# Transposing q and k by the DMA crossbar instead of TensorE, from the ninth unit on

## The chip, the core and the metric

The kernel runs on one core of one Trainium2 chip. A core has five engines with queues of their own, which meet at semaphores: TensorE (PE; its weight loads are PEld), VectorE (DVE), ScalarE (ACT), GpSimd (POOL) and SyncE (SP). Here SP issues all loads, ACT issues the stores of the results, and 16 DMA engines carry them out. An engine takes its instructions in the order of the program: one that waits holds up all behind it. The metric is the device time of one execution in microseconds (us), as the median of several runs.

## What is computed

Eight heads of retention (attention with a decay in place of the softmax), then a feed-forward block with a squared ReLU.

```python
scores = scale * np.matmul(q, k.transpose(0, 1, 3, 2))      # q, k, v: (8, 8, 576, 64) float32
gamma = 1.0 - 2.0 ** (-5.0 - np.arange(H))
Dmat = np.where(rel >= 0, gamma[:, None, None] ** rel, 0.0)  # rel = pos_i - pos_j
attn = np.matmul(scores * Dmat, v)
x = attn.transpose(0, 2, 1, 3).reshape(B * S, H * D)         # (4608, 512)
h = x @ w_in                                                 # (512, 2048)
r = np.maximum(h, 0.0)
out = (r * r) @ w_out                                        # (4608, 512) float32
```

## The kernel before

**Units.** A unit is 128 rows of the sequence with all 8 heads. A batch of 576 rows gives four full units, and the last 64 rows of two batches make one "tail" unit together: 36 units, nine for each pair of batches; unit 8 is the first tail. Heads go in pairs (NP = 4), so that a pair of 64 columns fills 128 partitions.

**What one unit does.** SP loads k, q and v as fp32 (L289, tails in two halves L292; five buffers). POOL casts k and q to fp16 (k16, q16; L338, L342) and multiplies v by its decay into vp (L347, four buffers, freed by the output matmuls four units back). For units 0 to 3 ACT casts q. PE transposes k and q, 128x128 at a time, four blocks each, into one PSUM tile psT (L374). ACT copies the k part to kT in two halves with zeros between, one for each head of a pair (L380, L383), and DVE copies the q part to qT (L387). From these PE makes the scores psc (L447, eight matmuls); DVE masks them into rT (L455). PE multiplies rT by vp and q by the running state R into psO (L479, L483). The state comes from k16 and vp (psS, L408) and two DVE steps (L422, L427). DVE scales psO into xT (L498).

**Feed-forward.** Units form groups of 1, 1, 2, 2, 2 and then 4. For each group PE makes ph (L526, 64 matmuls), ACT applies ReLU into rl (L534), DVE squares it into gT (L539), PE makes po (L556, 16 matmuls of 512 columns per unit), ACT copies po to o (L564) and issues the store (L570).

**What sets the order.** The class Schedule holds each step as a task with an engine, a key, an assumed duration, what it depends on, and the buffers that it takes and frees. `emit` plays these tasks through once while the program is built: at each moment a free engine takes the ready task with the lowest key. The order found is what each engine's queue then holds. The keys are due times in units of one feed-forward matmul; `base` is a unit's own, and L = 32 keys are one unit. A step of the retention part runs beside the feed-forward matmuls of the group before. SP's tasks all have key 0, in one chain. WARM matmuls (L235) keep PE running while the first loads come.

Each DMA raises one of eight completion counters, taken in turn by loads and stores alike in the order of the program, and it waits until the DMA that had its counter before has landed.

The names that the change touches: `kTs`, `kqs`, `fk`, `fq`, `fx2`, `ck` and `cq` (the casts), `tk` and `tq` (the transposes), `e0`, `e1`, `eq` (the copies out of PSUM), `transposed`, and the counts in `Schedule(dict(...))`.

Of the kernel before, what the change touches and what calls it, by code (L numbers as in the profile page):

```python
# [15 lines left out]
class Schedule:  # L16
# [85 lines left out]
def kernel(  # L102
# [9 lines left out]
    nc = tc.nc  # L112
# [33 lines left out]
    st_pool = ctx.enter_context(tc.tile_pool(name="st", bufs=6))  # L146
# [101 lines left out]
    zeroed = [[]]  # L248
    for i in range(1, NB):
        zeroed.append([add_gated("POOL", i - 1, "k", 1.5,  # L250
                                 lambda i=i: (zero_kT(nc.gpsimd, i), zero_vp(nc.gpsimd, i)))])

    def make_bdec():

# [74 lines left out]
    def add_ret(u):  # L329
# [2 lines left out]
        base = (u - len(us)) * L  # L332
        early = u < ahead
        tail = [tail_pool, tail_dec] if kind == "tail" else []

        def fk():
            t = tile_of["k16", u] = cast.tile([P, H * D], FP16, name="k16", tag="k16")
            nc.gpsimd.tensor_copy(out=t, in_=tile_of["k32", u].rearrange("p h d -> p (h d)"))  # L338

        def fq():  # L340
            t = tile_of["q16", u] = cast.tile([P, H * D], FP16, name="q16", tag="q16")
            (nc.scalar.copy if early else nc.gpsimd.tensor_copy)(  # L342
                out=t, in_=tile_of["q32", u].rearrange("p h d -> p (h d)"))

        def fv():
# [3 lines left out]
                in0=tile_of["v32", u].rearrange("p (n a) d -> p n a d", a=2),  # L349
                in1=vdec[kind].rearrange("p (n a o) -> p n a o", a=2, o=1).to_broadcast([P, NP, 2, D]),  # L350
                op=ALU.mult)
        ck = add("POOL", base - L, 0.73, fk, deps=[loaded["k", u]], acq=("k16",))
        if early:
            cq = add("ACT", base - L, 0.6, fq, deps=[loaded["q", u]], acq=("q16",))
        else:
            cq = add("POOL", base - L + 1, 0.62, fq, deps=[loaded["q", u]], acq=("q16",))
# [8 lines left out]
        def ft(i, src):  # L365
# [8 lines left out]
                    nc.tensor.transpose(tile_of["ps" + src[0], u][:, i, hp, :],  # L374
                                        tile_of[src, u][:, hp * P:(hp + 1) * P], ident)
            return f
        kT = kTs[u % NB]

        def fe0():
            nc.scalar.copy(out=kT[0:64, :, 0, :], in_=tile_of["psk", u][0:64, 0])  # L380
# [4 lines left out]
        def feq():  # L385
            t = tile_of["qT", u] = work.tile([P, NP, P], FP16, name="qT", tag="qT")
            nc.vector.tensor_copy(out=t, in_=tile_of["psq", u][:, 1])  # L387
        prev = [T["score", u - NB]] if u >= NB else zeroed[u]
        tk = add("PE", base - 17.6, 0.22, ft(0, "k16"), deps=[ck] if early else [ck, cq], acq=("psT",))
        tq = add("PE", base - 17.5, 0.22, ft(1, "q16"), deps=[cq, tk], acq=("psc",) if early else ())  # L390
        sched.free("q16", [tq])
        e0 = add("ACT", base - 15.5, 0.58, fe0, deps=[tk if early else tq] + prev)
        e1 = add("ACT", base - 15.4, 0.58, fe1, deps=[e0])

        eq = add("DVE", base - 15.3, 0.42, feq, deps=[tq] if early else [tq, e1], acq=("qT",))
        if early:
            sched.free("psT", [e0, e1])
            sched.free("psc", [eq])
        else:
            sched.free("psT", [e0, e1, eq])  # L400


        if kind == "full":
            def fs():
                ps = tile_of["psS", u] = ps_one.tile([P, NP, 2, D], FP32, name="psS", tag="psS")
                for hp in range(NP):
                    vo = vps[u % NB].rearrange("p n (a d) -> p n a d", d=64)[:, hp, 0:3:2, :]
                    nc.tensor.matmul(ps[:, hp], lhsT=tile_of["k16", u][:, hp * P:(hp + 1) * P], rhs=vo,  # L408
                                     start=True, stop=True)
            s = add("PE", base + 0.5, 0.22, fs, deps=[ck, cv], acq=("psS",))  # L410
            sched.free("k16", [s, tk])
            if c == 0:
                def fr():
                    Rn = tile_of["R", u] = st_pool.tile([P, NP, P], FP16, name="R", tag="R")
                    nc.vector.tensor_tensor(out=Rn, in0=tile_of["psS", u].rearrange("p n a d -> p n (a d)"),
                                            in1=bdec, op=ALU.mult)
                r = add("DVE", base + 1.5, 0.7, fr, deps=[s, made_bdec], acq=("R",))
                sched.free("psS", [r])
            else:
                def fr0():  # L420
                    tmp = tile_of["tmp", u] = work.tile([P, NP, P], FP32, name="stmp", tag="stmp", bufs=2)
                    nc.vector.tensor_tensor(out=tmp, in0=tile_of["psS", u].rearrange("p n a d -> p n (a d)"),  # L422
                                            in1=tile_of["R", u - 1], op=ALU.add)

                def fr():
                    Rn = tile_of["R", u] = st_pool.tile([P, NP, P], FP16, name="R", tag="R")
                    nc.vector.tensor_tensor(out=Rn, in0=tile_of["tmp", u], in1=bdec, op=ALU.mult)  # L427
                r0 = add("DVE", base + 1.5, 0.7, fr0, deps=[s, T["R", u - 1]])
                sched.free("psS", [r0])
                r = add("DVE", base + 1.6, 0.7, fr, deps=[r0], acq=("R",))  # L430
                T["Rread", u - 1].append(r0)
            T["R", u] = r
            T["Rread", u] = []
        else:
            sched.free("k16", [tk])


        sc = []
# [1 line left out]
        for half in range(2):  # L440
            for j in range(2):
                def f(half=half, j=j):
                    hp = 2 * half + j
                    if j == 0:
                        tile_of["psc", u, half] = ps_sc.tile([P, 2, 2, P], FP32, name="psc", tag="psc")
                    for a in range(2):
                        nc.tensor.matmul(tile_of["psc", u, half][:, j, a, :], lhsT=kT[:, hp, a, :],  # L447
                                         rhs=tile_of["qT", u][:, hp, :], start=True, stop=True)
                sc.append(add("PE", base + 5 + 2 * half + j + 0.6, 0.11, f, deps=[e0, e1, eq] + sc[-1:],
                              acq=("psc",) if j == 0 else ()))  # L450

            def fm(half=half):
                if half == 0:
                    tile_of["rT", u] = work.tile([P, NP, 2, P], FP16, name="rT", tag="rT")
                nc.vector.tensor_tensor(  # L455
                    out=tile_of["rT", u][:, 2 * half:2 * half + 2].rearrange("p n a i -> p (n a) i"),
                    in0=tile_of["psc", u, half].rearrange("p n a i -> p (n a) i"),
                    in1=mask[kind].rearrange("p (o i) -> p o i", o=1).to_broadcast([P, 4, P]),
                    op=ALU.mult)
# [13 lines left out]
        for hp in range(NP):  # L473
            def f(hp=hp):
# [6 lines left out]
                                     stop=(a == 1 and not inter))  # L481
                for n, (lo, hi, ru) in enumerate(inter):
                    nc.tensor.matmul(ps[:, hp, lo:hi], lhsT=tile_of["R", ru][:, hp, :],  # L483
                                     rhs=tile_of["qT", u][:, hp, lo:hi], start=False, stop=(n == len(inter) - 1))
# [134 lines left out]
```

## Time and profile before

| what | value |
|---|---|
| median of 3 runs (lowest to highest) | 336.01 us (335.69 to 336.94) |
| the profiled execution, its own time | 335.73 us |
| its span in the profile | 334.0 us |
| TensorE's granted clock | 1.00 in every stretch |
| transposes, L374 | 288 matmuls, 128x128 |
| scores, L447 | 288 matmuls, 128x128 |
| copies of kT, L380 and L383 | 36 and 36, 575 and 581 ns |
| copies of qT, L387 | 32 (and 4 more from another PSUM tile), 423 ns |
| casts of k and v's decay on POOL, L338 and L347 | 36 at 643 ns, 32 (full units) at 1049 ns |
| read from HBM, written | 36.70 MB, 9.44 MB |

The span is the time from the first to the last recorded event of the one profiled execution; the run's time is a little longer. A row of the timeline gives start, length, engine, line, operation, out<-in, size and count; a PE row's length has the last matmul's way through the array in it, so the start of the next row tells better when PE was free. In square brackets stands idle time of the engine ahead of the row, and what ended it. "SPq" is SP's queue: the time for which an issue held it.

### The profile page before, as it was taken

The numbers are of one execution on the slowest core, as the hardware profiler recorded it, in microseconds if no ns is written. First come the engines' busy times: TensorE is split into PE (matmuls) and PEld (weight loads), VectorE is DVE, ScalarE is ACT, GpSimd is POOL, SyncE is SP. The second block draws the span as 40 slices with busy tenths as digits, with TensorE's granted clock in tenths as the row PEclk, the third lists the DMA queues.
The fourth block names the chain that finished last, engine by engine and source line by source line (L and its number), as shares of the span: only waits on it lengthen the run. The fifth ranks groups of instructions, "written<-read, shape, count | busy, mean of one in ns | idle before, by whom it ended". The sixth has DMA issues, their size and how long they took to land.

```text
span 334.0 us, 6482 instructions
## 1 busy us (share of the span) xinstructions
PE 324.4 (97%) x2528; PEld 194.4 (58%) x2528; DVE 192.5 (58%) x367; ACT 159.9 (48%) x273; POOL 98.7 (30%) x141
## 2 busy tenths in 40 slices
PE   5999999899999999999999999999999999999996
PEld 2679655777755555555555555555555555554444
DVE  2596436887848843774388447843686357623500
ACT  4458843643446523662366226632663256414611
POOL 6834475657322222322222222312222110000000
PEclk9999999999999999999999999999999999999999
DMA  9999999999959958435544565453000120011013
GB/s 176 222 386 386 305 252 224 225 205 252 222 132 232 208 125 208 105 73 148 149 104 90 131 154 124 97 127 95 32 2 0 65 63 0 3 65 63 0 42 86
DMA packets 122158, 46.56 MB, mean 139 GB/s; under 512 B 113296, under 2 KB 113552, under 8 KB 122128
## 3 DMA queue, kind: packets, MB, share of 16 engines
q1 hardware_dynamic: 116736, 36.71, 50.1%
q10 hardware_dynamic: 5392, 9.44, 8.4%
q8 instruction: 20, 0.33, 0.4%
q14 instruction: 10, 0.08, 0.1%
HBM read 36.70 MB, written 9.44 MB: 138 GB/s over the span
## 4 chain that ended last, share of the span: by engine, by line
PE 86%; SPq 7%; DVE 3%; DMA 1%; issue 1%; POOL 0%; ACT 0%; POOLq 0%
PE ph L526 34%; PE po L556 33%; SPq L289 6%; PE psO L479 4%; PE psc L447 4%; PE psT L374 4%; PE warm L235 3%; PE psS L408 2%; PE psO L483 2%; DMA q<-in_q_dram 1%; SPq L292 1%; DVE rT L455 1%; DVE R L427 1%; DVE stmp L422 1%; POOL q L342 0%
## 5 line engine op out<-in xcount | busy, mean ns | idle before, releaser
L556 PE MATMUL po<-w_out,gT 128*128 128x512 f16 (+1 forms) x592 | 146.8, 373 | 0.8 <-POOL w_out L314 0.8
L526 PE MATMUL ph<-xT,w_in 128*128 128x512 f16 (+2 forms) x768 | 140.6, 326 | 0.0
L534 ACT ACTIVATE rl<-ph 128x512 f16<-128x512 f32 x144 | 85.6, 597 | 47.3 <-PE ph L526 42.8
L526 PEld LDWEIGHTS <-w_in 128*128 128x128 f16 x768 | 66.1, 98 | 39.0
L539 DVE TENSOR_TENSOR gT<-rl 128x512 f16<-128x512 f16 x144 | 71.1, 500 | 27.1 <-ACT rl L534 25.4
L556 PEld LDWEIGHTS <-gT 128*128 128x128 f16 x592 | 55.2, 98 | 42.2 <-issue 1.0
L380 ACT COPY kTb<-psT 64x512 f16<-64x512 f16 x36 | 20.7, 575 | 63.6 <-PE psT L374 59.8
L564 ACT COPY o<-po 128x512 f32<-128x512 f32 (+1 forms) x37 | 21.3, 575 | 56.1 <-PE po L556 55.7
L455 DVE TENSOR_TENSOR rT<-psc,mask_full 128x512 f16<-128x512 f32 x64 | 41.8, 684 | 6.7 <-PE psc L447 6.3
L347 POOL TENSOR_TENSOR vp<-v,vdec_full 128x512 f16<-128x512 f32 x32 | 33.6, 1049 | 34.4 <-PE psO L483 24.9
L342 POOL CAST q<-q 128x512 f16<-128x512 f32 x32 | 21.3, 666 | 68.4 <-PE psT L374 24.7
L338 POOL CAST k<-k 128x512 f16<-128x512 f32 x36 | 23.2, 643 | 42.5 <-issue 20.0
L479 PEld LDWEIGHTS <-vp 128*128 128x128 f16 x288 | 25.4, 98 | 16.3 <-issue 1.2
L479 PE MATMUL psO<-rT,vp 128*128 128x128 f16 x288 | 33.9, 219 | 0.4 <-DVE rT L455 0.2
L387 DVE COPY qT<-psT 128x512 f16<-128x512 f16 x32 | 13.5, 423 | 35.0 <-ACT kTb L383 34.9
L447 PEld LDWEIGHTS <-kTb 128*128 128x128 f16 x288 | 23.7, 98 | 15.3 <-issue 0.3
L447 PE MATMUL psc<-qT,kTb 128*128 128x128 f16 x288 | 31.5, 219 | 0.0
L422 DVE TENSOR_TENSOR stmp<-psS,R 128x512 f32<-128x512 f32 x24 | 16.5, 689 | 25.2 <-PE psS L408 25.0
L498 DVE TENSOR_TENSOR xT<-psO,gam_full 128x512 f16<-128x512 f32 x32 | 22.1, 690 | 9.5 <-PE psO L483 5.3
L483 PE MATMUL psO<-qT,R 128*128 128x128 f16 (+1 forms) x128 | 22.6, 212 | 0.0
L383 ACT COPY kTb<-psT 64x512 f16<-64x512 f16 x36 | 20.9, 581 | 0.6
L235 PE MATMUL warm<-junk,ident 128*128 128x512 f16 x48 | 15.0, 425 | 3.7 <-DVE junk L230 3.7
(57 smaller groups left out, 159.5 us busy)
## 6 DMA issues: line engine op xcount, KB each, us to landing
k<-in_k_dram SPq DMA_DIRECT2D x32, 256.0 KB, 4.7
q<-in_q_dram SPq DMA_DIRECT2D x32, 256.0 KB, 4.7
v<-in_v_dram SPq DMA_DIRECT2D x32, 256.0 KB, 4.8
out_dram<-o ACTq DMA_DIRECT2D x31, 256.0 KB, 2.1
wi<-in_moe_w_in_dram SPq DMA_DIRECT2D x4, 1024.0 KB, 10.7
wo<-in_moe_w_out_dram SPq DMA_DIRECT2D x4, 1024.0 KB, 9.3
out_dram<-o ACTq DMA_DIRECT2D x10, 128.0 KB, 2.4
k<-in_k_dram SPq DMA_DIRECT2D x8, 128.0 KB, 3.9
```

The source lines that it names most:

```text
L235: nc.tensor.matmul(warm_ps[0], lhsT=ident, rhs=junk, start=True, stop=True)
L338: nc.gpsimd.tensor_copy(out=t, in_=tile_of["k32", u].rearrange("p h d -> p (h d)"))
L347: nc.gpsimd.tensor_tensor(out=vo, in0=tile_of["v32", u].rearrange("p (n a) d -> p n a d", a=2), in1=vdec[kind].rearrange("p (n a o) -> p n ...
L447: nc.tensor.matmul(tile_of["psc", u, half][:, j, a, :], lhsT=kT[:, hp, a, :], rhs=tile_of["qT", u][:, hp, :], start=True, stop=True)
L455: nc.vector.tensor_tensor(out=tile_of["rT", u][:, 2 * half:2 * half + 2].rearrange("p n a i -> p (n a) i"), in0=tile_of["psc", u, half].re ...
L479: nc.tensor.matmul(ps[:, hp, :], lhsT=vps[u % NB][:, hp, a * 64:a * 64 + P], rhs=tile_of["rT", u][:, hp, a, :], start=(a == 0), stop=(a == ...
L483: nc.tensor.matmul(ps[:, hp, lo:hi], lhsT=tile_of["R", ru][:, hp, :], rhs=tile_of["qT", u][:, hp, lo:hi], start=False, stop=(n == len(inte ...
L498: nc.vector.tensor_tensor(out=tile_of["x", us[0]][:, :, s * P:(s + 1) * P], in0=tile_of["psO", u], in1=gam[kind], op=ALU.mult)
L526: nc.tensor.matmul(tile_of["ph", g, fb][:, j, :], lhsT=w_in16[:, m, fi * P:(fi + 1) * P], rhs=tile_of["x", us[0]][:, m, :], start=(m == 0) ...
L534: nc.scalar.activation(out=t, in_=tile_of["ph", g, fb], func=ACTF.Relu)
L539: nc.vector.tensor_tensor(out=t, in0=rl, in1=rl, op=ALU.mult)
L556: nc.tensor.matmul(tile_of["po", u, lo], lhsT=tile_of["g", g, fi // nf][:, fi % nf, s * P:(s + 1) * P], rhs=w_out16[:, fi, lo:hi], start=( ...
```

## The change

The program of units 0 to 7 stays, but for some buffer counts. From unit 8 on (XBAR = 8):

- POOL writes k twice: into a tile kq of 12 blocks of 128 columns, where blocks 0 to 7 hold the four pairs of k, each pair twice, once with the second and once with the first head's 64 columns left at zero; and as before into k16, for the state. It writes q into blocks 8 to 11. There are three kq tiles; DVE zeroes their k parts once at the start.
- SP issues one DMA that transposes all 12 blocks into a tile kqT (three buffers). It depends on both casts. Its key is -1, ahead of the loads, its assumed duration 2.0.
- psT and the copies kT and qT are gone; the scores and the state's part of the output read kqT.
- The casts of unit u wait for the transpose of unit u-3, which reads the same kq.
- Buffers: kT 4 to 3, R 6 to 5, rT 3 to 2, q16 4 to 2. The warm-up matmuls read the first kq instead of a tile of their own.

```diff
-    kTs = [const.tile([P, NP, 2, P], FP16, name=f"kTb{i}") for i in range(NB)]
+    NT = 3
+    kTs = [const.tile([P, NP, 2, P], FP16, name=f"kTb{i}") for i in range(NT)]
...
+    NK = 3
+    kqs = [const.tile([P, 3 * NP, P], FP16, name=f"kq{i}") for i in range(NK)]
+    nc.vector.memset(kqs[0][:, 0:2 * NP], 0.0)
     zero_kT(nc.vector, 0)
     zero_vp(nc.vector, 0)
+    for t in kqs[1:]:
+        nc.vector.memset(t[:, 0:2 * NP], 0.0)
...
+    XBAR = 8
-    sched = Schedule(dict(ff=3, psc=2, psT=1, psS=1, psO=1, ld=5, wst=4, k16=4, q16=4,
-                          qT=3, rT=3, x=3, rl=3, o=3, R=6))
+    sched = Schedule(dict(ff=3, psc=2, psT=1, psS=1, psO=1, ld=5, wst=4, k16=4, q16=2,
+                          qT=3, rT=2, x=3, rl=3, o=3, R=5, kqT=3))
...
-    junk = const.tile([P, 512], FP16, name="junk")
-    nc.vector.memset(junk, 0.0)
+    junk = kqs[0][:, 0:NP].rearrange("p n c -> p (n c)")
...
+        xbar = u >= XBAR
+        kq = kqs[u % NK]
         def fk():
+            if xbar:
+                nc.gpsimd.tensor_copy(
+                    out=kq[:, 0:2 * NP].rearrange("p (n a) (b d) -> p n (a b) d", a=2, d=64)[:, :, 0:4:3, :],
+                    in_=tile_of["k32", u].rearrange("p (n a) d -> p n a d", a=2))
             t = tile_of["k16", u] = cast.tile([P, H * D], FP16, name="k16", tag="k16")
...
         def fq():
+            if xbar:
+                nc.gpsimd.tensor_copy(out=kq[:, 2 * NP:].rearrange("p n c -> p (n c)"),
+                                      in_=tile_of["q32", u].rearrange("p h d -> p (h d)"))
+                return
...
-        ck = add("POOL", base - L, 0.73, fk, deps=[loaded["k", u]], acq=("k16",))
+        old = [T["kq", u - NK]] if u - NK >= XBAR else []
+        ck = add("POOL", base - L, 1.4 if xbar else 0.73, fk, deps=[loaded["k", u]] + old, acq=("k16",))
...
+        if xbar:
+            def fx2():
+                t = tile_of["kqT", u] = work.tile([P, 3 * NP, P], FP16, name="kqT", tag="kqT")
+                nc.sync.dma_start_transpose(out=t, in_=kq.rearrange("p n c -> p (n c)"))
+            T["kq", u] = add("SP", -1, 2.0, fx2, deps=[ck, cq], acq=("kqT",))
+            transposed = [T["kq", u]]
+        else:
...
+            transposed = [e0, e1, eq]
+
+        def k_T(hp, a):
+            return tile_of["kqT", u][:, 2 * hp + a, :] if xbar else kT[:, hp, a, :]
+
+        def q_T(hp):
+            return tile_of["kqT", u][:, 2 * NP + hp, :] if xbar else tile_of["qT", u][:, hp, :]
...
-                        nc.tensor.matmul(tile_of["psc", u, half][:, j, a, :], lhsT=kT[:, hp, a, :],
-                                         rhs=tile_of["qT", u][:, hp, :], start=True, stop=True)
-                sc.append(add("PE", base + 5 + 2 * half + j + 0.6, 0.11, f, deps=[e0, e1, eq] + sc[-1:],
+                        nc.tensor.matmul(tile_of["psc", u, half][:, j, a, :], lhsT=k_T(hp, a),
+                                         rhs=q_T(hp), start=True, stop=True)
+                sc.append(add("PE", base + 5 + 2 * half + j + 0.6, 0.11, f, deps=transposed + sc[-1:],
...
-        sched.free("qT", [outs[-1]])
+        sched.free("kqT" if xbar else "qT", [outs[-1]])
```

The queues move at two places. On SP, before, from the tail unit 8 (k32_958 and so on) to unit 10 (k32_1084 and so on) there are loads alone:

```order
L292 DMA k32_958<-in_k_dram 64x8x64 x2
L292 DMA q32_980<-in_q_dram 64x8x64 x2
L292 DMA v32_1000<-in_v_dram 64x8x64 x2
L289 DMA k32_1011<-in_k_dram 128x8x64
L289 DMA q32_1029<-in_q_dram 128x8x64
L289 DMA v32_1057<-in_v_dram 128x8x64
L289 DMA k32_1084<-in_k_dram 128x8x64
L289 DMA q32_1109<-in_q_dram 128x8x64
L289 DMA v32_1138<-in_v_dram 128x8x64
```

and now, in the same place, with the transposes of units 8, 9 and 10 (kqT_1056, kqT_1119, kqT_1274):

```order
L299 DMA v32_1001<-in_v_dram 64x8x64 x2
L296 DMA k32_1013<-in_k_dram 128x8x64
L296 DMA q32_1030<-in_q_dram 128x8x64
L410 DMA_TRANSPOSE kqT_1056<-kq2_151 128x12x128
L296 DMA v32_1095<-in_v_dram 128x8x64
L410 DMA_TRANSPOSE kqT_1119<-kq0_149 128x12x128
L296 DMA k32_1166<-in_k_dram 128x8x64
L296 DMA q32_1183<-in_q_dram 128x8x64
L296 DMA v32_1209<-in_v_dram 128x8x64
L296 DMA k32_1223<-in_k_dram 128x8x64
L296 DMA q32_1252<-in_q_dram 128x8x64
L410 DMA_TRANSPOSE kqT_1274<-kq1_150 128x12x128
```

Unit 8's transpose stands ahead of v of unit 9, unit 9's directly behind it and ahead of all loads of unit 10.

On PE, before, from the transposes of unit 8 (psT_1038) to its scores (psc_1106), rows that repeat left out:

```order
L374 LDWEIGHTS k16_1007
L374 MATMUL psT_1038<-ident_98,k16_1007 128x128
L374 LDWEIGHTS q16_1022
L374 MATMUL psT_1038<-ident_98,q16_1022 128x128
L526 LDWEIGHTS w_in16_96
L526 MATMUL ph_1050<-xT_915,w_in16_96 128x256
L447 MATMUL psc_1060<-qT_986,kTb2_148 128x128
L447 MATMUL psc_1072<-qT_986,kTb2_148 128x128
L526 MATMUL ph_1077<-xT_915,w_in16_96 128x256
L526 MATMUL ph_1096<-xT_915,w_in16_96 128x256
L447 LDWEIGHTS kTb0_146
L447 MATMUL psc_1106<-qT_1094,kTb0_146 128x128
```

and now, from the transposes of unit 7 (psT_1098), which stand ahead of the scores of unit 8 (psc_1142, psc_1149):

```order
L393 LDWEIGHTS k16_956
L393 MATMUL psT_1098<-ident_98,k16_956 128x128
L393 LDWEIGHTS q16_972
L393 MATMUL psT_1098<-ident_98,q16_972 128x128
L559 MATMUL ph_1111<-xT_916,w_in16_96 128x256
L512 MATMUL psO_1127<-rT_1077,vp2_144 128x128
L516 LDWEIGHTS R_945
L516 MATMUL psO_1127<-qT_987,R_945 128x128
L559 MATMUL ph_1135<-xT_916,w_in16_96 128x256
L480 LDWEIGHTS kqT_1056
L480 MATMUL psc_1142<-kqT_1056 128x128
L480 MATMUL psc_1149<-kqT_1056 128x128
```

Unit 8 has no transposes on PE any more, and its scores have moved behind unit 7's transposes, more of ph, and half of unit 6's output (psO_1127).

More of the change, by code (lines that the diff above doesn't have):

```diff
@@ L145 @@
     x_pool = ctx.enter_context(tc.tile_pool(name="x", bufs=3))
-    st_pool = ctx.enter_context(tc.tile_pool(name="st", bufs=6))
+    st_pool = ctx.enter_context(tc.tile_pool(name="st", bufs=5))
     g_pool = ctx.enter_context(tc.tile_pool(name="g", bufs=32))
@@ L250 @@
         zeroed.append([add_gated("POOL", i - 1, "k", 1.5,
-                                 lambda i=i: (zero_kT(nc.gpsimd, i), zero_vp(nc.gpsimd, i)))])
+                                 lambda i=i: (zero_kT(nc.gpsimd, i) if i < NT else None, zero_vp(nc.gpsimd, i)))])
     def make_bdec():
@@ L340, in fq @@
         def fq():
-            t = tile_of["q16", u] = cast.tile([P, H * D], FP16, name="q16", tag="q16")
+            if xbar:
+                nc.gpsimd.tensor_copy(out=kq[:, 2 * NP:].rearrange("p n c -> p (n c)"),
+                                      in_=tile_of["q32", u].rearrange("p h d -> p (h d)"))
+                return
+            t = tile_of["q16", u] = cast.tile([P, H * D], FP16, name="q16", tag="q16", bufs=2)
             (nc.scalar.copy if early else nc.gpsimd.tensor_copy)(
@@ L355, in add_ret @@
         else:
-            cq = add("POOL", base - L + 1, 0.62, fq, deps=[loaded["q", u]], acq=("q16",))
+            cq = add("POOL", base - L + 1, 0.62, fq, deps=[loaded["q", u]] + old, acq=() if xbar else ("q16",))
         cv = add("POOL", base - L + 2, 1.1, fv, deps=[loaded["v", u]] + tail +
@@ L376, in ft @@
             return f
-        kT = kTs[u % NB]
+        kT = kTs[u % NT]
         def fe0():
@@ L387, in feq @@
             nc.vector.tensor_copy(out=t, in_=tile_of["psq", u][:, 1])
[L388 to L398, printed above, removed]
-        else:
-            sched.free("psT", [e0, e1, eq])
+        if xbar:
[4 more added lines that the diff above has]
+            transposed = [T["kq", u]]
+        else:
+            prev = [T["score", u - NT]] if u >= NT else zeroed[u]
+            tk = add("PE", base - 17.6, 0.22, ft(0, "k16"), deps=[ck] if early else [ck, cq], acq=("psT",))
+            tq = add("PE", base - 17.5, 0.22, ft(1, "q16"), deps=[cq, tk], acq=("psc",) if early else ())
+            sched.free("q16", [tq])
+            e0 = add("ACT", base - 15.5, 0.58, fe0, deps=[tk if early else tq] + prev)
+            e1 = add("ACT", base - 15.4, 0.58, fe1, deps=[e0])
+            eq = add("DVE", base - 15.3, 0.42, feq, deps=[tq] if early else [tq, e1], acq=("qT",))
+            if early:
+                sched.free("psT", [e0, e1])
+                sched.free("psc", [eq])
+            else:
+                sched.free("psT", [e0, e1, eq])
+            transposed = [e0, e1, eq]
[3 more added lines that the diff above has]
+            return tile_of["kqT", u][:, 2 * NP + hp, :] if xbar else tile_of["qT", u][:, hp, :]
         if kind == "full":
@@ L410, in add_ret @@
             s = add("PE", base + 0.5, 0.22, fs, deps=[ck, cv], acq=("psS",))
-            sched.free("k16", [s, tk])
+            sched.free("k16", [s] if xbar else [s, tk])
             if c == 0:
@@ L434, in add_ret @@
         else:
-            sched.free("k16", [tk])
+            sched.free("k16", [ck if xbar else tk])
         sc = []
@@ L453, in fm @@
                 if half == 0:
-                    tile_of["rT", u] = work.tile([P, NP, 2, P], FP16, name="rT", tag="rT")
+                    tile_of["rT", u] = work.tile([P, NP, 2, P], FP16, name="rT", tag="rT", bufs=2)
                 nc.vector.tensor_tensor(
@@ L483, in f @@
                     nc.tensor.matmul(ps[:, hp, lo:hi], lhsT=tile_of["R", ru][:, hp, :],
-                                     rhs=tile_of["qT", u][:, hp, lo:hi], start=False, stop=(n == len(inter) - 1))
+                                     rhs=q_T(hp)[:, lo:hi], start=False, stop=(n == len(inter) - 1))
             outs.append(add("PE", base + 18.5 + hp, 0.16, f,
```

## The prediction

> **What bounds the kernel now.** I read the page's engine shares first, then its chain of waits.
>
> ```profile
> span 334.0 us, 6482 instructions
> PE 324.4 (97%) x2528; PEld 194.4 (58%) x2528; DVE 192.5 (58%) x367; ACT 159.9 (48%) x273; POOL 98.7 (30%) x141
> ...
> PE 86%; SPq 7%; DVE 3%; DMA 1%; issue 1%; POOL 0%; ACT 0%; POOLq 0%
> PE ph L526 34%; PE po L556 33%; SPq L289 6%; PE psO L479 4%; PE psc L447 4%; PE psT L374 4%; PE warm L235 3%; PE psS L408 2%; PE psO L483 2%; DMA q<-in_q_dram 1%; SPq L292 1%; DVE rT L455 1%; DVE R L427 1%; DVE stmp L422 1%; POOL q L342 0%
> ```
>
> TensorE is busy for 97% of the span and makes up 86% of the chain. The loads (SPq L289 and L292) hold 7% of it, and psT at L374, the work that is to go, holds 4%. A busy PE need not be a full one, so the second look is at time by stretches and at who waits for whom.
>
> ```profile
> 50.00:60.00 10.00, 8.44 (x72) 5.11 (x70) 7.30 (x11) 3.51 (x6) 6.07 (x8) 1.00 1.06 222
> 60.00:70.00 10.00, 10.00 (x114) 8.73 (x112) 7.70 (x16) 7.55 (x13) 6.36 (x8) 1.00 1.34 227
> 140.00:180.00 40.00, 40.00 (x300) 22.59 (x298) 25.73 (x47) 20.18 (x35) 9.70 (x13) 1.00 0.53 125
> 260.00:300.00 40.00, 40.00 (x288) 22.25 (x287) 21.58 (x41) 17.48 (x30) 1.65 (x2) 1.00 0.10 34
> ```
>
> The columns are length, then busy PE, PEld, DVE, ACT, POOL, then the granted clock, DMA share and GB/s. PE idles in the first 60 us, while loads limit it, and then not at all up to 300 us; the clock is 1.00 throughout. DMA is full up to 70 us, half full at 140 to 180 and nearly empty after 260.
>
> ```profile
> ACT rl L534 <- PE ph L526: 42.8, 106, 2.4
> POOL vp L347 <- PE psO L483: 24.9, 16, 1.8
> PE psT L374 <- POOL q L342: 1.3, 1, 1.3
> ```
>
> The waits (total, times, longest) say the same: ACT and POOL wait for PE, and in this region PE waits once, 1.3 us, for a q cast. So after 60 us the time is the sum of what PE is given.
>
> **What goes: the transposes.** Eight per unit, four of k and four of q, here those of unit 9.
>
> ```profile
> 66.89 0.39 PE L374 MATMUL psT<-ident,k 128*128 128x128 f16 x4
> 67.12 0.39 PE L374 MATMUL psT<-ident,q 128*128 128x128 f16 x4
> 67.34 0.93 PE L526 MATMUL ph<-xT,w_in 128*128 128x256 f16 x7
> ...
> 290.23 0.39 PE L374 MATMUL psT<-ident,k 128*128 128x128 f16 x4
> 290.45 0.39 PE L374 MATMUL psT<-ident,q 128*128 128x128 f16 x4
> 290.67 1.03 PE L556 MATMUL po<-w_out,gT 128*128 128x512 f16 x4
> ```
>
> From start to start they hold PE 67.34 - 66.89 = 0.45 us in the first case, 290.67 - 290.23 = 0.44 in the last. Units 8 to 35 are 28 units: 28 x 0.445 = **12.5 us**. All of it lies where PE never idles, so all of it counts.
>
> That this region is packed shows in the period of a group of four units:
>
> ```profile
> 234.54 0.86 PE ph L526 x4
> ...
> 269.10 0.86 PE ph L526 x4
> ```
>
> 34.56 us for four units is 8.64 per unit; without the transposes 8.2.
>
> **What else goes.** Per unit two ACT copies and one DVE copy:
>
> ```profile
> L380 ACT COPY kTb<-psT 64x512 f16<-64x512 f16 x36 | 20.7, 575 | 63.6 <-PE psT L374 59.8
> L387 DVE COPY qT<-psT 128x512 f16<-128x512 f16 x32 | 13.5, 423 | 35.0 <-ACT kTb L383 34.9
> ```
>
> That is 28 x (0.575 + 0.581) = 32 us of ACT and 28 x 0.423 = 12 us of DVE. Both engines wait for PE, so I count nothing for it. It does make sure that they stay out of the way at the shorter period: the 8.2 us hold less of their work than the 8.64 did. Fewer buffers (rT 3 to 2, R 6 to 5, kT 4 to 3) take some of that room back; I cost them at nothing, since the writers of these tiles are ACT and DVE, which the rows above show busy for 20 and 26 of 40 us; gone, that cover would turn into waits of PE for rT or R.
>
> **What is added on POOL.** One more k cast per unit, into the zero-padded copy. A k cast takes 0.61 us. POOL is 30% busy and waits for PE, and in the load-limited stretch the cast fits before q lands:
>
> ```profile
> 57.15 0.61 POOL L338 CAST k<-k 128x512 f16<-128x512 f32 x1
> 58.73 1.06 POOL L342 CAST q<-q 128x512 f16<-128x512 f32 x1 [0.97 <-DMA q<-in_q_dram]
> 63.10 0.62 POOL L342 CAST q<-q 128x512 f16<-128x512 f32 x1 [0.57 <-DMA q<-in_q_dram]
> ```
>
> These are units 8 and 9: 0.97 us idle before q8's cast cover the extra 0.61. Cost nothing.
>
> **What is added on SP.** One transpose per unit, 128 x 1536 fp16 = 384 KB, in the queue that also issues every load. No row shows such a transfer. The nearest are the loads:
>
> ```profile
> 58.05 0.37 SPq L289 DMA_DIRECT2D k<-in_k_dram  x1
> 58.53 0.65 SPq L289 DMA_DIRECT2D q<-in_q_dram  x1
> 59.27 1.12 SPq L289 DMA_DIRECT2D v<-in_v_dram  x1
> ...
> 65.18 1.09 SPq L289 DMA_DIRECT2D q<-in_q_dram  x1
> ...
> k<-in_k_dram SPq DMA_DIRECT2D x32, 256.0 KB, 4.7
> out_dram<-o ACTq DMA_DIRECT2D x31, 256.0 KB, 2.1
> ```
>
> A 256 KB load in a row of loads holds the queue 1.09 us and lands 4.7 us after issue; a store of that size lands after 2.1. Let t be the time for which a transpose holds the queue. Lower end: 0.37, the shortest issue. Upper end: nothing behind it moves until it has landed, 1.5 x 4.7 = 7.05 us for 1.5 times the bytes. I take the row nearest in kind, a load among loads, scaled by bytes: **t = 1.5 x 1.09 = 1.64 us**, landing 4.7 + 0.55 = 5.25 us after issue.
>
> The Trainium skill, "DMA: Bandwidth & Descriptors", section "Latency and other measured facts", gives 261 GB/s for a transposing DMA; as an estimate that is 1.5 us for 384 KB, and no run here shows it yet.
>
> At t = 1.64 a unit holds SP for 3 x 1.09 + 1.64 = 4.9 us of the 8.2 that PE needs: hidden, once units run ahead. A transpose also waits on SP for its casts, and behind it wait the loads of units further on. Later in the kernel it waits as well for a kqT buffer, freed by the last output matmul three units back; the scores that read it stand some two units later in PE's order, 16 us, against 5.25.
>
> **Where it shows: units 8 to 10**, which have no lead yet.
>
> ```profile
> 58.14 0.39 PE L374 MATMUL psT<-ident,k 128*128 128x128 f16 x4
> 59.85 0.40 PE L374 MATMUL psT<-ident,q 128*128 128x128 f16 x4 [1.32 <-POOL q L342]
> ...
> 62.71 0.39 PE L447 MATMUL psc<-qT,kTb 128*128 128x128 f16 x4
> 62.94 0.60 PE L526 MATMUL ph<-xT,w_in 128*128 128x256 f16 x4
> 63.37 0.39 PE L374 MATMUL psT<-ident,k 128*128 128x128 f16 x4
> ```
>
> Unit 8's transposes now cause the 1.32 us wait; it goes. Its scores start at 62.71. In the new order PE has four more groups of four ph matmuls ahead of them (0.43 each, 62.94 to 63.37), unit 7's transposes (0.45) and half of an output (0.32), less unit 8's transposes (0.45): 2.05 us. So PE comes to them at 62.71 - 1.32 + 2.05 = 63.4. The transpose can be issued when q8 is cast, 58.73 + 1.06 = 59.8, and lands at 65.05: a **new wait of 1.7 us** (0 with a store's 2.1 to land, 3.5 with 7.05). Unit 9: q9 is cast at 63.7, lands at 69.0; PE comes to its scores 4.5 us after unit 8's, at 63.4 + 1.7 + 4.5 = 69.6: no further wait. Unit 10: after unit 9's transpose, SP issues k10 and q10 by 66.5; q10 lands 4.7 later, is cast at 71.8, its transpose lands at 77.1; PE comes at 69.6 + 9.8 = 79.4. From there the lead grows by 8.2 - 4.9 us a unit.
>
> **The sum**, against the profiled execution: span 334.0 - 12.5 - 1.3 + 1.7 = 321.9. Around the span lie 335.73 - 334.0 = 1.7 us: **323.6 us**. That execution is 0.3 below the median of 336.01.
>
> **Rivals.**
>
> *A: the transposes run one after the other at a price that the queue can't hide; slower.* From 59.8 on SP has 28 transposes and 79 loads (v9 and units 10 to 35), 79 x 1.09 = 86 us. The last unit's scores start at 296.31, which leaves 37.7 us to the end:
>
> ```profile
> 296.31 0.27 PE L447 MATMUL psc<-qT,kTb 128*128 128x128 f16 x2
> ```
>
> 59.8 + 86 + 28t + 37.7 = 183.5 + 28t. Up to t = 4.9 PE hides it; from 5.4 the kernel is slower than before; at the upper end, 7.05, it takes 381 + 1.7 = 383 us. For it: a transposing write has no row here, and DMA is full in the ramp. Against it: 384 KB in the store's and the load's rows take far less, and DMA is half free from 140 us on.
>
> The Trainium skill, "VectorE: DVE Perf Modes", section "The three transpose paths", gives 1309 ns for a 128x128 transpose by the crossbar against 390 ns on TensorE, and its rules name TensorE where PSUM will do. Twelve blocks one after the other would be an estimated 15.7 us a unit, and by rival A's sum 625 us. The trace differs on TensorE's price, 0.45 / 8 = 56 ns; for the crossbar no run here shows it yet.
>
> *B: the ramp.* The same order, with t = 4.9 and landing after 7.05: unit 8's scores wait 3.5 us; unit 9's transpose is issued at 65.8 behind v9 and lands at 72.8 against 67.9; q10 is issued by 72, its transpose goes at 77.2 and lands at 84.2, where PE would come at 77.8 with no waits before. The largest lateness counts, 6.4: 334.0 - 12.5 - 1.3 + 6.4 + 1.7 = 328.3. For it: loads already limit this stretch, and SP stands still while a transpose waits for its casts. Against it: it needs three times the load's price.
>
> *C: PE does not close up.* Another chain (ph to rl to gT) or the shared completion counters of loads, stores and transposes set the 8.64 us period: 335.7, the profiled execution's own time. Against it: ACT waits 106 times for ph and has half its time free.
>
> **Chances.** Forecast (321 to 326) 0.63; B and its neighbourhood (326 to 331) 0.20; C 0.05; A 0.12. The range 321.0 to 329.5 leaves out A, C and the end of B. A measurement of this kernel can tell about 0.5% from no change. Faster by more than that: 0.63 + 0.20 = 0.83; within it 0.05; slower 0.12.
>
> **What would show it.** Right: psT rows only for units 0 to 7, a group period near 32.8 us, one short PE wait at unit 8's scores, about 1.7 us, its releaser the transpose. Wrong: a transpose's issue-to-landing far over 5 us; PE waiting for kqT again and again after 100 us (A); PE waits of several us between 63 and 80 (B); a period that stays at 34.6 with ACT or DVE named (C).

## The result, and the profile after

| kernel | median | runs | ratio to before, 95% interval |
|---|---|---|---|
| before | 336.06 us (335.69 to 336.94) | 4 | |
| changed | 323.59 us (322.91 to 324.27) | 4 | 0.9625 [0.9598, 0.9653] |

Faster by 12.5 us; the forecast was 323.6 us. The profiled execution of the changed kernel took 324.27 us, with a span of 322.6. From its page, the first lines, the shares of its chain of waits, and the load queue's row, with the row of before behind it:

```profile
span 322.6 us, 5955 instructions
PE 312.5 (97%) x2304; PEld 182.1 (56%) x2304; DVE 183.9 (57%) x341; ACT 128.8 (40%) x217; POOL 115.7 (36%) x167
...
PE 85%; DMA 7%; DVE 4%; issue 1%; POOL 1%; ACT 1%; POOLq 0%; SPq 0%
...
q1 hardware_dynamic: 160640, 47.72, 74.2%
...
q1 hardware_dynamic: 116736, 36.71, 50.1%
```

PE has 2528 - 2304 = 224 matmuls fewer, eight for each of 28 units, and is still 97% busy: what follows has moved up. ACT fell from 48 to 40%. The queue of the loads now moves 47.72 MB for 36.71, and its packets take 74.2% of the DMA engines' time, before 50.1% (how much of the rise is the transposes' own is not shown: where DMAs crowd, a share goes above 1, as the 1.23 below).

The chain in order of time gives the period of a group of four units, from one group's first ph to the next one's:

```profile
160.82 0.86 PE ph L559 x4
...
193.59 0.86 PE ph L559 x4
```

32.77 us against 34.56: 0.447 per unit, just the transposes' 0.445. PE's timeline at the scores of units 8 (all eight matmuls) and 9 (the first two); in brackets idle time and what ended it:

```profile
63.11 0.60 PE L559 MATMUL ph<-xT,w_in 128*128 128x256 f16 x4
65.11 0.62 PE L480 MATMUL psc<-kqT 128*128 128x128 f16 x8 [1.41 <-DMA kqT<-kq]
...
69.61 0.28 PE L480 MATMUL psc<-qT,kTb 128*128 128x128 f16 x2
70.35 0.29 PE L480 MATMUL psc<-kqT 128*128 128x128 f16 x2 [0.47 <-DMA kqT<-kq]
```

PE comes to unit 8's scores at 63.5 and waits 1.41 us for the transpose; at unit 9 it waits 0.47. PE has no other wait for kqT in the kernel. The transposes themselves, first the answer for their line (ns of queue held, shortest, median, longest; then issue to landing), then SP's timeline:

```profile
L410 SPq DMA_TRANSPOSE kqT<-kq x28: 1287/2454/3564, 60.6 to 265.5; - x28
...
DMA to landing us min/median/max: 3.7/4.7/7.1
```

```profile
59.97 0.52 SPq L296 DMA_DIRECT2D q<-in_q_dram  x1
60.59 2.72 SPq L410 DMA_TRANSPOSE kqT<-kq  x1
...
64.50 1.87 SPq L410 DMA_TRANSPOSE kqT<-kq  x1
...
97.81 3.51 SPq L410 DMA_TRANSPOSE kqT<-kq  x1
101.36 0.58 SPq L296 DMA_DIRECT2D v<-in_v_dram  x1
101.98 0.58 SPq L296 DMA_DIRECT2D k<-in_k_dram  x1
102.61 1.06 SPq L296 DMA_DIRECT2D q<-in_q_dram  x1
103.71 0.91 SPq L296 DMA_DIRECT2D v<-in_v_dram  x1
104.67 1.82 SPq L299 DMA_DIRECT2D k<-in_k_dram  x2
106.60 2.49 SPq L410 DMA_TRANSPOSE kqT<-kq  x1
...
159.06 2.45 SPq L410 DMA_TRANSPOSE kqT<-kq  x1
...
200.14 1.45 SPq L410 DMA_TRANSPOSE kqT<-kq  x1
```

From 97.81 to 159.06 SP issues seven units' worth of transposes with four or five loads between each two, and hardly rests: 61.25 / 7 = 8.75 us a unit, more than PE's 8.2. Here loads run ahead, and the lead that they build is used by nobody yet. At 200.14 the queue is quiet, and a transpose holds it 1.45 us. The stretches (PE, PEld, DVE, ACT, POOL busy, clock, DMA share, GB/s) show the same on the DMA engines:

```profile
100.00:140.00 40.00, 40.00 (x270) 21.52 (x269) 26.31 (x47) 16.26 (x28) 17.07 (x24) 1.00 1.23 217
140.00:190.00 50.00, 50.00 (x338) 26.82 (x337) 29.70 (x51) 16.62 (x29) 23.08 (x31) 1.00 1.14 229
190.00:222.00 32.00, 32.00 (x222) 17.32 (x221) 18.86 (x33) 11.39 (x20) 10.63 (x14) 1.00 0.87 173
```

DMA is full up to 190 us, where before it was half free from 140 on. PE never idles in any of them.

### The profile page after: what moved, and what is told of

It is laid out like the page before. It is cut to its first block, busy times and chain, and to the rows that moved or that the text cites. A ratio compares the mean times of both kernels' runs of the same rounds, so it can differ in the third digit from the quotient of the medians.

```text
span 322.6 us, 5955 instructions
## 1 busy us (share of the span) xinstructions
PE 312.5 (97%) x2304; PEld 182.1 (56%) x2304; DVE 183.9 (57%) x341; ACT 128.8 (40%) x217; POOL 115.7 (36%) x167
## 3 DMA queue, kind: packets, MB, share of 16 engines
q1 hardware_dynamic: 160640, 47.72, 74.2%
## 4 chain that ended last, share of the span: by engine, by line
PE 85%; DMA 7%; DVE 4%; issue 1%; POOL 1%; ACT 1%; POOLq 0%; SPq 0%
PE po L589 36%; PE ph L559 33%; PE psO L512 4%; PE psc L480 4%; PE warm L242 3%; DMA wo<-in_moe_w_out_dram 3%; PE psS L441 2%; DMA kqT<-kq 2%; PE psO L516 2%; DMA out_dram<-o 1%; DVE rT L488 1%; DMA k<-in_k_dram 1%; DVE R L460 1%; DVE stmp L455 1%; PE psT L393 0%
## 5 line engine op out<-in xcount | busy, mean ns | idle before, releaser
L589 PE MATMUL po<-w_out,gT 128*128 128x512 f16 (+1 forms) x592 | 144.5, 373 | 1.0 <-POOL w_out L321 1.0
L559 PE MATMUL ph<-xT,w_in 128*128 128x512 f16 (+2 forms) x768 | 138.0, 326 | 0.0
L348 POOL CAST kq<-k 128x512 f16<-128x512 f32 x28 | 19.2, 684 | 42.3 <-DMA kqT<-kq 21.4
L356 POOL CAST kq<-q 128x512 f16<-128x512 f32 x28 | 19.5, 696 | 28.9 <-DMA kqT<-kq 23.0
L480 PEld LDWEIGHTS <-kqT 128*128 128x128 f16 x224 | 19.3, 98 | 16.0 <-DMA kqT<-kq 2.3
L480 PE MATMUL psc<-kqT 128*128 128x128 f16 x224 | 26.1, 219 | 1.9 <-DMA kqT<-kq 1.9
L460 DVE TENSOR_TENSOR R<-stmp,bdec 128x512 f16<-128x512 f32 x24 | 18.4, 765 | 0.8
L242 PE MATMUL warm<-kq,ident 128*128 128x512 f16 x48 | 15.5, 438 | 3.3 <-DVE kq L218 3.3
L516 PE MATMUL psO<-kqT,R 128*128 128x128 f16 (+1 forms) x104 | 17.9, 211 | 0.0
L441 PEld LDWEIGHTS <-k 128*128 128x128 f16 x128 | 9.8, 98 | 6.2
```

The source lines that it names most:

```text
L242: nc.tensor.matmul(warm_ps[0], lhsT=ident, rhs=junk, start=True, stop=True)
L559: nc.tensor.matmul(tile_of["ph", g, fb][:, j, :], lhsT=w_in16[:, m, fi * P:(fi + 1) * P], rhs=tile_of["x", us[0]][:, m, :], start=(m == 0) ...
L589: nc.tensor.matmul(tile_of["po", u, lo], lhsT=tile_of["g", g, fi // nf][:, fi % nf, s * P:(s + 1) * P], rhs=w_out16[:, fi, lo:hi], start=( ...
```

## The experiments

The theory: after the ramp the time is the sum of PE's work, so the transposes' 12.5 us count in full, and all else is hidden except a short wait at units 8 and 9. The rivals: the gain came from ACT and DVE, from other buffers, or from the ramp; or the transposes are far from hidden.

**1. TensorE's transposes back, as well as the DMA's.**

```diff
             transposed = [T["kq", u]]
+            def fspare():
+                ps = ps_one.tile([P, 2, NP, P], FP16, name="psT", tag="psT")
+                for i in range(2):
+                    for hp in range(NP):
+                        nc.tensor.transpose(ps[:, i, hp, :], tile_of["k16", u][:, hp * P:(hp + 1) * P] if i == 0
+                                            else kq[:, 2 * NP + hp, :], ident)
+            tk = add("PE", base - 17.6, 0.44, fspare, deps=[ck, cq])
...
```

The lines left out make k16's buffer wait for these transposes too.

> The changed kernel, with the eight TensorE transposes of each unit from 8 on done as well, into psT, which nobody reads. DMA transpose stays, copies out of PSUM stay away. Theory (the time is the sum of PE's work): 28 x 0.445 = 12.5 us come back, 323.6 + 12.5 = 336.1 us, between 334.5 and 337. Rival (what paid was the relief of ACT and DVE, not of PE): 323.6 to 325.

Measured: 338.96 us (1.008 [1.0058, 1.0102] of before). The whole gain is gone, and the time is 2.9 us above the sum, and above the expected range. The table of PE's waits names waits that this kernel makes itself, for the PSUM tile and for the casts:

```profile
PE psT L418 <- DVE qT L406: 1.8, 1, 1.8
...
PE psT L418 <- POOL kq L356: 1.1, 2, 0.8
```

They are 2.9 us, but that they equal the excess is chance: this kernel has no wait for kqT, which cost the changed kernel 1.9. In the profiled execution the span is 336.4 us, 13.8 above the changed kernel's; 12.5 of transposes + 2.9 - 1.9 = 13.5 explains that. The median is 15.4 above, and what makes up the other 1.6 us is not shown. Between the theories the run still decides: with the relief of ACT and DVE kept, nothing is gained.

**2. The copies of ACT and DVE back, out of kqT.**

```diff
+            def fspare0():
+                nc.scalar.copy(out=kT[0:64, :, 0, :], in_=tile_of["kqT", u][0:64, 0:NP])
+            def fspare1():
+                nc.scalar.copy(out=kT[64:128, :, 1, :], in_=tile_of["kqT", u][64:128, 0:NP])
+            def fspareq():
+                t = work.tile([P, NP, P], FP16, name="qT", tag="qT")
+                nc.vector.tensor_copy(out=t, in_=tile_of["kqT", u][:, 2 * NP:])
+            e0 = add("ACT", base - 15.5, 0.58, fspare0, deps=[T["kq", u]])
+            e1 = add("ACT", base - 15.4, 0.58, fspare1, deps=[e0])
+            eq = add("DVE", base - 15.3, 0.42, fspareq, deps=[T["kq", u], e1])
...
```

The lines left out keep the kqT buffer until these copies have read it.

> The changed kernel, with the two ACT copies and the DVE copy of each unit from 8 on done as well, out of kqT into buffers that nobody reads; no TensorE transposes. Theory (PE's sum): ACT and DVE have room, 323.6 us, within 1.6. Rival (relief of ACT and DVE paid): most of the 12.5 us come back, 330 to 336.

Measured: 334.74 us (0.9953 [0.9933, 0.9973]). The rival's number; but not by its reason, as ACT's timeline shows:

```profile
135.59 1.08 ACT L580 ACTIVATE rl<-ph 128x512 f16<-128x512 f32 x2 [0.77 <-PE psc L493]
142.13 0.62 ACT L415 COPY kTb<-kqT 64x512 f16<-64x512 f16 x1 [5.45 <-DMA kqT<-kq]
142.65 0.59 ACT L580 ACTIVATE rl<-ph 128x512 f16<-128x512 f32 x1
```

The copy stands at the head of ACT's queue for 5.45 us, until its transpose has landed. Behind it stands a ReLU whose ph was there all along, and PE, which needs that PSUM buffer back, stops for 4.73 us:

```profile
143.29 1.64 PE L572 MATMUL ph<-xT,w_in 128*128 128x512 f16 x4 [4.73 <-ACT rl L580]
```

PE's waits for rl come to 7.9 us in all. The mean granted clock of this execution was 0.989, which over 335.2 us is another 3.7 us (the last section has the rows). Together that is 11.6 of the 12.6 us by which its span is longer than the changed kernel's. That the copies' wait and not their length started this is still only argued here; the ninth run parts the two.

**3. The new buffer counts without the crossbar.** `XBAR = 36`.

> The changed kernel's buffer counts (kT 3, R 5, rT 2, q16 2) and zeroing at the start, but every unit transposed on TensorE. Theory (buffers cost nothing): 336.1 us, within 1.0. Rival (fewer buffers add waits that the change had to pay for): 338 or more, and then the crossbar's own gain is larger than 12.5.

Measured: 336.12 us (0.9994 [0.9968, 1.0019]). The smaller buffer counts cost nothing that this can tell; its interval reaches from 1.1 us faster to 0.6 us slower.

**4. A longer planned distance.** The order is made with 6.0 us from a transpose to its readers in place of 2.1.

```diff
-            T["kq", u] = add("SP", -1, 2.0, fx2, deps=[ck, cq], acq=("kqT",))
+            T["kq", u] = add("SP", -1, 2.0, fx2, after=6.0, deps=[ck, cq], acq=("kqT",))
```

> The changed kernel, planned with 6.0 us instead of 2.1 from the end of a transpose to its readers, so that PE's order puts the scores of unit 8 behind 3.8 us more of its other work, and those of unit 9 behind 4 us more. Theory (PE waits 1.4 and 0.5 us there for the transposes, which land some 4.5 us after issue): both waits go, 323.6 - 1.9 = 321.7 us. Rival (the loads behind limit the stretch, and PE waits elsewhere as long): 323.6 or more.

Measured: 322.01 us (0.9586 [0.957, 0.9602]). PE's timeline at unit 8's scores:

```profile
66.11 1.03 PE L589 MATMUL po<-w_out,gT 128*128 128x512 f16 x4
66.98 0.61 PE L480 MATMUL psc<-kqT 128*128 128x128 f16 x8
67.77 0.38 PE L441 MATMUL psS<-vp,k 128*128 128x128 f16 x4 [0.18 <-POOL vp L365]
```

No bracket at psc: the transpose is there when PE comes, 3.5 us later than in the changed kernel, having done other work first. The two waits, 1.9 us together, were real and were a matter of order. This kernel beats the changed one by 1.6 us, though the two intervals overlap by a hair.

**5 and 6. More to transpose.** Behind each unit's transpose one (two) more of the 8 k blocks, into kT buffers. This overwrites the kT of unit 7 before its last four scores have read it, and in run 6 that of unit 6 as well, so these units are computed from other data.

```diff
                 nc.sync.dma_start_transpose(out=t, in_=kq.rearrange("p n c -> p (n c)"))
+                nc.sync.dma_start_transpose(out=kTs[u % NT].rearrange("p n a c -> p (n a) c"),
+                                            in_=kq[:, 0:2 * NP].rearrange("p n c -> p (n c)"))
```

> The changed kernel, with a second DMA transpose behind each unit's own: 8 blocks of kq again, into a kT buffer that is no longer used. 20 blocks per unit instead of 12. In the changed kernel a unit's three loads and transpose took SP 5.9 to 6.2 us where it never rested, so a transpose's share is 2.7. Theory (the queue's price adds up per block and is hidden up to 8.2 us a unit): 3.3 + 2.7 x 20/12 = 7.8 us, just hidden; 323.6 plus a later ramp, 324 to 329 us. Rival (a fixed price per transpose, not per block): 3.3 + 5.4 = 8.7 us a unit, so the queue sets the time: 183.5 + 28 x 5.4 = 335 and 1.7 around it, 336 us.

> As the run before, with two such extra transposes of 8 blocks: 28 blocks per unit. Theory: 3.3 + 2.7 x 28/12 = 9.6 us a unit, more than PE's 8.2: the queue becomes the bound, 183.5 + 28 x 6.3 = 360 and 1.7 around it, some 362 us, with PE waiting for kqT all through. Rival (the price is that of the quiet end, 1.44 us of hold per 12 blocks; the rest was waiting): 3.3 + 3.4 = 6.7 us a unit, hidden, 324 to 330 us.

Measured: 334.86 us (0.9967 [0.9936, 0.9998]) and 367.76 us (1.0921 [1.0863, 1.0978]). Neither can be used as it stands, by the first row of run 5's table of PE's waits:

```profile
PE psc L481 <- DMA kTb<-kq: 6.6, 1, 6.6
```

Unit 7's scores had to wait for the kT that was being overwritten, which is not the queue's price. Run 6 has 9.6 us of such waits beside 22.4 us for kqT, so its 367.76 against some 362 expected is no clean check of the queue as bound either. Runs 10 and 12 leave these waits out.

**7. Half the units.** `XBAR = 22`.

> The changed kernel with the crossbar from unit 22 on instead of 8: 14 units instead of 28. Theory (0.445 us for each unit, nothing fixed): 336.1 - 14 x 0.445 = 329.9 us, with the ramp's wait for q8 back in it and none for kqT. Rival (a good part of the gain came from the ramp or from the buffers): over 332, or under 328.

Measured: 330.52 us (0.9824 [0.9782, 0.9866]). 14 units give 5.6 us, 0.40 each; 28 gave 12.5, 0.445 each. The interval of this run is some 4.5 to 7.3 us, so a gain in proportion (6.2) fits, and a fixed part of more than some 2 us does not.

**8. More units.** `XBAR = 4`.

> The changed kernel with the crossbar from unit 4 on: 32 units. Theory (in the stretch that loads limit, each transpose holds SP ahead of loads that PE waits for): 4 x 0.445 = 1.8 us less for PE, but units 4 to 8 arrive 5 to 10 us later: 326 to 332 us. Rival (the lead is enough there too): 323.6 - 1.8 = 321.8 us.

Measured: 327.48 us (0.9743 [0.9703, 0.9783]), 3.9 more than from unit 8 on. PE's timeline, the rows with a wait:

```profile
55.51 0.62 PE L480 MATMUL psc<-kqT 128*128 128x128 f16 x8 [1.08 <-DMA kqT<-kq]
...
71.84 0.40 PE L480 MATMUL psc<-kqT 128*128 128x128 f16 x4 [1.58 <-DMA kqT<-kq]
...
81.18 0.62 PE L480 MATMUL psc<-kqT 128*128 128x128 f16 x8 [0.63 <-DMA kqT<-kq]
...
84.72 0.38 PE L441 MATMUL psS<-vp,k 128*128 128x128 f16 x4 [1.16 <-POOL vp L365]
```

The time lies in the theory's range. PE waits for kqT, and for vp, whose v is loaded behind a transpose in SP's queue; the waits go on for 30 us. They account for 1.5 of the 3.9 us (5.2 us of waits against 1.9, less 1.8 for four more units without transposes on PE); the rest could not be assigned.

**9. The copies again, waiting for nothing.** From unit 11 on; source w_in16 in place of kqT.

```diff
+            if u >= 11:
+                def fspare0():
+                    nc.scalar.copy(out=kT[0:64, :, 0, :], in_=w_in16[0:64, :, 0:P])
+                def fspare1():
+                    nc.scalar.copy(out=kT[64:128, :, 1, :], in_=w_in16[64:128, :, 0:P])
+                def fspareq():
+                    nc.vector.tensor_copy(out=kT[0:64, :, 1, :], in_=w_in16[0:64, :, 0:P])
...
```

The lines left out place the three copies in the order as in run 2. In the profile ACT's take 618 and 615 ns and DVE's 389, near the old 575, 581 and 423.

> The changed kernel, with two ACT copies and a DVE copy of the old sizes (64x512 fp16) per unit from 11 on, at the places that the order gives to the old ones, but out of w_in16, which is there since the start: they take ACT's and DVE's time and wait for nothing. Theory (in the second run the copies cost time because they stood in ACT's queue waiting for kqT, with the ReLU behind them, and not by their length): 323.6 us, within 1.6. Rival (their length counts, the relief of ACT and DVE was part of the gain): 25 of 28 units of what the second run lost, 11.1 x 25/28 = 10, so 333.5.

Measured: 324.14 us (0.9655 [0.9634, 0.9675]), no difference from the changed kernel that can be told. ACT does the work, here in the stretch from 100 to 140, where it had 16.26 us in the changed kernel:

```profile
100.00:140.00 40.00, 40.00 (x270) 21.51 (x268) 29.17 (x52) 22.32 (x38) 17.57 (x24) 1.00 1.22 215
```

So the length of ACT's and DVE's copies is not paid for; what run 2 paid for was the wait in the queue.

**10 and 12. More to transpose, from unit 11 on.** As 5 and 6, with `if u >= 11:` ahead of the extra transposes.

> As the run with 8 more blocks per unit, but only from unit 11 on, so that no kT buffer is written that unit 7 still reads (its 6.6 us wait for that buffer is not the queue's). 20 blocks per unit. Theory (per block, hidden up to 8.2 us a unit): 3.3 + 2.7 x 20/12 = 7.8 us, hidden: 323.6 to 326 us. Rival (a price per transpose): 8.7 us a unit, 25 x 0.5 = 12 us more than the lead can take up, 330 to 336.

> As the run with 16 more blocks per unit, but only from unit 11 on. 28 blocks per unit. Theory: 3.3 + 2.7 x 28/12 = 9.6 us a unit against PE's 8.2: the queue sets the time over most of 25 units, 25 x 1.4 = 35 us more less the lead of some 10 us: 340 to 360 us, with PE waiting for kqT. Rival (16 more blocks are hidden too): under 330.

Measured: 334.17 us (0.9947 [0.9918, 0.9975]) and 356.25 us (1.057 [1.0529, 1.0611]). Run 12 came out in the theory's range, with PE waiting for kqT; its row among PE's waits (total, times, longest):

```profile
PE psc L483 <- DMA kqT<-kq: 23.2, 15, 4.1
```

Not all of it is the wait: the mean granted clock of that execution was 0.975, which over 354.4 us is some 9 us, of 31.8 by which the span is longer than the changed kernel's.

Run 10 gave the rival's number, so 8 more blocks were not hidden. SP's timeline, the units' own transposes alone:

```profile
123.39 3.82 SPq L410 DMA_TRANSPOSE kqT<-kq  x1
...
134.03 2.97 SPq L410 DMA_TRANSPOSE kqT<-kq  x1
...
144.19 2.97 SPq L410 DMA_TRANSPOSE kqT<-kq  x1
...
164.24 3.25 SPq L410 DMA_TRANSPOSE kqT<-kq  x1
```

These are 40.85 us for four units, 10.2 each, where the expectation said 7.8. It had reckoned three loads per transpose; between these stand five. In the changed kernel the same stretch runs at 8.75, so 8 blocks cost 1.5 us, 0.18 a block. That is nearer to a price per block; a price per transpose would have made it some 2.5 to 3 us. So the run came out at the rival's number without the rival's reason: the theory's sum started from the wrong base. With 10.2 against 8.2 the lead is gone by 141 us:

```profile
141.08 0.51 PE L482 MATMUL psc<-kqT 128*128 128x128 f16 x6 [2.30 <-DMA kqT<-kq]
```

**11. The longer distance and two units more.** Run 4's edit with `XBAR = 6`.

> The fourth run's planning (6.0 us from a transpose to its readers) with the crossbar from unit 6 on: 30 units. Theory (a planned distance removes the wait also two units earlier): 322.0 - 2 x 0.445 = 321.1 us. Rival (the two transposes delay the loads of units 8 to 10, as they did from unit 4 on, where each unit cost about 1 us instead of gaining 0.445): 323 to 325.

Measured: 325.26 us (0.9673 [0.9634, 0.9712]), from 323.17 to 328.41. Three executions with a granted clock of 1.00 took 323.2 to 323.8 us, the other three, at 0.990 to 0.995, 326.7 to 328.4. Even the first three are 1.2 to 1.8 us above run 4, where 0.9 should have been gained: the rival's range. The profiled execution, the longest, has one wait of 5.5 us for vp at the state's matmuls; unit 9's v, issued at 68.80, stood on SP behind unit 8's transpose, issued at 66.37. Whether the others have that wait stays open.

## Why the prediction was right, by its steps

- **The transposes, 12.5 us.** Right. The period fell by 0.447 us a unit; half the units gave 5.6 us, where 6.2 lies within the interval (run 7); with the transposes back on PE the gain was gone (run 1).
- **ACT and DVE relieved, nothing.** Right (run 9). The reason is the one given, that they wait for PE. Run 2 shows its limit: a short copy that waits at the head of the queue holds up what stands behind it, and that is paid for.
- **Buffers, nothing.** Right (run 3).
- **The extra cast on POOL, nothing.** POOL went from 30 to 36% busy and no wait of PE names it after unit 8. Unit 8's transpose was issued 0.8 us later than the sum had it, 60.59 for 59.8. POOL's cast of its q ended at 60.07 (59.03 + 1.04), 0.3 late; its k had landed later too, so that is not shown to be the extra cast. The rest is SP's own queue, which the sum left out: the load of unit 9's q, issued at 59.97, held it to 60.49.
- **The transpose's price.** Mis-sized: 1.64 us forecast, 2.45 held in the median, 1.45 in the quiet end. The landing was 4.7 us in the median, where 5.25 was forecast. For 384 KB, 1.45 us is 271 GB/s, if the time held is taken for the transfer's; among loads it is 160 GB/s. The Trainium skill's "DMA: Bandwidth & Descriptors", section "Latency and other measured facts", gives 261 GB/s for a transpose with a non-contiguous middle dimension, an estimated 1.5 us here, and 350 to 400 GB/s for a contiguous one. The trace is near the first where the queue is quiet, and below both among loads.
- **"4.9 us of the 8.2", "the lead grows by 8.2 - 4.9 us a unit".** This step failed. Three loads per transpose is the mean over the kernel, but in the order five stand between each two for some seven units, and with some 3 us for a transpose (2.49 to 3.51) that came to 8.75. The lead shrank there by 7 x 0.55 = 3.9 us, where the sum let it grow by 7 x 3.3. It lasted all the same, since PE does not wait for kqT there. Run 10 shows how near the edge was: 8 blocks more, and the kernel is at 334. That this step did no harm to the forecast is in part luck.
- **"DMA is half free from 140 us on."** Wrong in the changed kernel: the share is 1.23 and 1.14 in the two stretches up to 190 us. The argument against rival A was weaker than it looked.
- **The new wait, 1.7 us at unit 8 and none at unit 9.** It was 1.41 and 0.47; run 4 removes them and wins 1.6. At unit 8 two errors cancel, which is luck: the transpose was issued 0.8 us late, but landed 4.5 us after issue (65.11 - 60.59) and not 5.25, so at 65.1 as forecast. At unit 9 it landed 5.85 us after issue (70.35 - 64.50), 0.6 more than forecast.
- **The sum.** In the profiled execution the span fell by 11.4 and not 12.1: 0.2 by the wait, 0.5 in pieces that I could not assign. That the median came out at the very tenth is luck to that extent.
- **Rival A** is a real mechanism: run 12 is past its point, at 356. Its sum is not borne out in size: with run 12's holds (28 of 2.63 us, 25 each of 1.42 and 1.51 on average) it gives 59.8 + 86 + 147 + 37.7 + 1.7 = 332, and the clock's 9 us are not enough to close the gap. The Trainium skill, "VectorE: DVE Perf Modes", section "The three transpose paths", gives 1309 ns for one 128x128 transpose by the crossbar; that is not what a block costs in one long transpose. All twelve landed within 3.7 to 7.1 us, and 8 blocks more cost 1.5. So the figure is no reason against the change here. **Rival B** did not happen here; from unit 4 on (run 8) waits of its kind appear. **Rival C** is out by the period.

## What to carry to other kernels

Where an engine never idles, as TensorE here after the ramp, work taken from it counts in full, and work taken from engines that wait for it counts nothing. Before moving work to a queue, count in the order what stands between two uses of it in each stretch, not on the mean over the kernel: the margin here was 3 us a unit by the mean, and less than nothing for seven units. And the distance that a planner assumes should cover the landing under load; here 6.0 in place of 2.1 was worth 1.6 us for one number.

## What the runs showed of the hardware that I had not expected

A wait of PE can cost more than its length. The clock granted to TensorE was 1.00 in every stretch of the changed kernel, with its waits of up to 1.41 us. In run 2, after the wait of 4.73 us that ended at 143.29, the stretches read:

```profile
140.00:144.00 4.00, 0.71 (x3) 0.32 (x3) 0.43 (x1) 1.82 (x4) 1.78 (x3) 0.94 1.34 194
144.00:148.00 4.00, 4.00 (x18) 1.91 (x17) 2.37 (x6) 2.16 (x4) 1.22 (x2) 0.63 1.52 183
```

and in run 10, with the wait of 2.30 us that ended at 141.08:

```profile
140.00:144.00 4.00, 2.92 (x15) 1.46 (x16) 1.72 (x4) 0.60 (x1) 1.88 (x3) 0.71 1.30 223
```

A mean clock of 0.63 and 0.71 over 4 us is 1.5 and 1.2 us of full speed lost, on top of the wait; with the microseconds beside these stretches it is 1.7 in both. In run 10 that closes the sum: 8.3 us of waits for kqT against 1.9, and 1.7 by the clock, come to 8.1, and its span is 8.0 us longer than the changed kernel's. Its spread goes with the clock too: the three executions with a mean clock of 0.993 to 0.995 took 332.4 to 332.8 us, the seven at 0.989 to 0.990 took 333.6 to 336.1.

The length of the wait alone does not decide it. In run 2 a wait of 1.69 us, with one of 0.24 close behind it, was followed by a lower clock, in run 7 one of 1.58 us too (0.58 in the mean from 60 to 64 us), and in run 10 one of 3.18 us was not:

```profile
104.78 1.02 PE L572 MATMUL ph<-xT,w_in 128*128 128x512 f16 x4 [1.69 <-ACT rl L580]
104.00:108.00 4.00, 2.98 (x9) 1.08 (x9) 2.61 (x6) 2.98 (x7) 2.28 (x3) 0.75 1.16 226
...
170.78 0.51 PE L482 MATMUL psc<-kqT 128*128 128x128 f16 x6 [3.18 <-DMA kqT<-kq]
170.00:174.00 4.00, 3.22 (x24) 1.81 (x25) 2.39 (x4) 1.20 (x2) 2.96 (x4) 1.00 1.21 205
```

The Trainium skill, "TensorE: Matmul & The Clock Gate", section "Why this matters for your kernels", says that idle gaps of more than some 3 us bring the clock down to half. The traces agree on the half (0.50 from 142 to 145 us in run 10), but not on the length: 1.69 us was enough once, and 3.18 us was not. What decides it stays open here.
